# Opening of an attention-plus-MLP kernel: loads of two chunks at once, all scores of group 0 ahead of the MLP, and idle products between

## The chip, the cores and the metric

The kernel runs on one core of a Trainium2 chip. The metric is the device time of one execution in microseconds (us). Three executions of the kernel before gave a median of 213.64 us (213.39 to 215.62). The engines are named as the profile names them: PE is TensorE (its matrix products and transposes), PEld its weight loads, ACT is ScalarE, DVE is VectorE, POOL is GpSimd, SP is SyncE. POOL and SP issue the DMAs here: POOL every load, SP every store and every transposing DMA.

## The reference

Decaying linear attention over 4 batches, 8 heads, 768 positions and a head dimension of 64, followed by an MLP with an exact GELU over the 3072 tokens (512 to 2048 to 512). All inputs are float32.

```python
for b in range(nb):                       # blocks of 64 positions
    intra = einsum('bhic,bhjc->bhij', qb, kb) * Dmask
    intra = einsum('bhij,bhjd->bhid', intra, vb)
    inter = einsum('bhid,bhde->bhie', qb * lam_pow, kv_state)
    out[:, :, sl] = intra + inter
    kv_state = lam_block * kv_state + einsum('bhsd,bhse->bhde', kb * rev_pow, vb)
x = out.transpose(0, 2, 1, 3).reshape(B * S, H * D)
return gelu_exact(x @ w_in) @ w_out
```

## The kernel before

**Tiles.** The sequence is cut into 6 groups of 128 positions. A group has 4 chunks, one for each batch, so chunk n belongs to group n // 4. A chunk holds 128 positions of all 8 heads. The attention output of a group is a tile `x_t` of 128x4x512 (features by tokens), 128 columns for each chunk. The MLP of a group multiplies it with 16 slices of `w_in` (4 products of 128x512 each, one GELU on ACT behind them), and then with `w_out` (16 parts, "p0" to "p15", of 4 products each, for four chunks). All multiplications are in bf16; the loads turn float32 into bf16 on the way.

**Group 0 and the others.** Group 0 has no state before it. A chunk of it is made by `transposed` (k and q, each 16 small PE transposes into a PSUM bank and one copy out, by ACT or DVE, into `kqT`), `scores0` (8 products and two DVE multiplications with the mask), `outputs0` (8 products with v) and `empty` (one DVE multiplication into the chunk's columns of `x_t`). For the groups after it, `visit(f, d)` issues the scores and state products of chunk d, interleaved with the outputs of chunk f. Chunks 4 to 7 are transposed on PE (`both_transposed`), chunks from 8 on by transposing DMAs that SP issues (`dma_transposes`, L252 for k and L253 for q, called by `request`).

**The order is written out by hand.** `ask` (L126) issues loads on POOL's queue in the order of a string: "k0" is k of chunk 0, "v0" is v of chunks 0 and 1, "i0-3" slices 0 to 2 of `w_in` (two DMAs), "o0-4" a quarter of `w_out` (one DMA), "V1" v of all of group 1 (four DMAs). The loads of POOL count their landings on eight semaphores in turn, so that each load waits until the eighth load ahead of it has landed. The first string is at L143. `keep_warm(n)` issues n products of 128x512 on a tile of zeros, whose result nobody reads. `mlp(g, n2, n3)` returns the MLP of a group as named blocks: "a", "b" and "m" blocks compute slices of `w_in`, the slices below n3 without the columns of the group's last chunk, which "l" blocks add; `run_blocks` (L494) runs them in order and, ahead of a block, whatever the plan names for it.

**The opening of group 0** stands at L501 to L526: the first three chunks are transposed, chunks 0 and 1 are finished and the scores of chunk 2 made. The rest of group 0's attention hangs on MLP blocks (L565): `third` at b0 (outputs of chunk 2, transposes of chunk 3), scores of chunk 3 at m2, its outputs at m4. `ahead_of_group_1` at m5 issues POOL work: `decay_v(4)` (`vd`, the decayed values of chunk 4, which needs V1), loads k7 and q7, `decay_v(5)`, two copies, `decay_v(6)`, `decay_v(7)`, and then the loads V2, k8, q8, k9, q9. `visit(None, 4)` is at p6.

**Group 1** follows with the plan of `plan_of(1)` (L603 to L624; n is 8 there): `request(9)` at a0, stores of group 0's results and `request(10, 11)` at m5, `visit(None, 8)` at m7, `visit(8, 9)` at m12, `visit(9, 10)` at p2. `request(8)` stands at p14 of group 0. SP works its queue in order: the transposes of chunk 8, two stores, the transposes of chunk 9, two stores, those of chunks 10 and 11.

Of the kernel before, what the change touches and what calls it, by code (L numbers as in the profile page):

```python
# [9 lines left out]
BF16 = mybir.dt.bfloat16  # L10
ALU = mybir.AluOpType
ACT = mybir.ActivationFunctionType
# [3 lines left out]
def kernel(  # L16
# [28 lines left out]
    qkv_pool = ctx.enter_context(tc.tile_pool(name="qkv", bufs=10))  # L45
# [19 lines left out]
    raw = {}  # L65
    dram = dict(q=q, k=k, v=v)

    def load(n, name):
        g, b = n // B, n % B
        t = raw[n, name] = qkv_pool.tile([128, H, D], BF16, tag=name, name=f"{name}_t", bufs=10)  # L70
        nc.gpsimd.dma_start(t, dram[name][b, :, g * C:(g + 1) * C, :].rearrange("h si d -> si h d"))  # L71

    def load_pairs(n, name):
        g, b = n // B, n % B
        if n < B:
            t = raw[n, "kq"] if (n, "kq") in raw else qkv_pool.tile([128, H, 2, D], BF16, tag="kq", name="kq_t", bufs=B)
            raw[n, "kq"] = t
            t = t[half("kq".index(name))]  # L80
        else:
            t = raw[n, name] = qkv_pool.tile([64, H, 2, D], BF16, tag="q2", name="q2_t", bufs=B)
        src = dram[name][b, :, g * C:(g + 1) * C, :].rearrange("h (p j) d -> p h (j d)", j=2)
        nc.gpsimd.dma_start(t.rearrange("p h j d -> p h (j d)"), src)  # L84

    def load_parity(n):

        t = qkv_pool.tile([128, 2 * H, D], BF16, tag="v", name="v_t", bufs=2)
        src = v[n:n + 2, :, :C, :].rearrange("b h (p j) d -> j p (b h) d", j=2)
        for j in range(2):  # L90
            nc.gpsimd.dma_start(t[half(j)], src[j])  # L91
        for i in range(2):
            raw[n + i, "v"] = t[:, i * H:(i + 1) * H, :]

    def load_blocks(g):

        t = raw["group", g] = qkv_pool.tile([128, 2, B * HP, D], BF16, tag="vg", name="vg_t", bufs=3)
        src = v.rearrange("b (hp hi) s d -> hi s (b hp) d", hi=2)
        for u in range(2):
            for hi in range(2):  # L100
                s = g * C + u * L
                nc.gpsimd.dma_start(t[half(hi), u], src[hi, s:s + L])  # L102
# [4 lines left out]
    pos = consts.tile([128, 1], F32)  # L107
# [18 lines left out]
    def ask(items):  # L126

        for item in items.split():
            name, at = item[0], item[1:]
            if name in "kqv":  # L130
                n = int(at)
                if name == "v":
                    load_parity(n)
                elif n < B or n < 2 * B and name == "q":
                    load_pairs(n, name)
                else:
                    load(n, name)
            elif name == "V":
                load_blocks(int(at))
            else:  # L140
                (load_w_in if name == "i" else load_w_out)(*(int(x) for x in at.split("-")))

    ask("k0 q0 k1 q1 v0 k2 q2 i0-3 v2 k3 q3 i3-5 i5-8 i8-12 i12-16 o0-4 k4 q4 o4-8 V1 o8-12 k5 q5 o12-16 k6 q6")  # L143

    idle = consts.tile([128, 512], BF16)
    nc.vector.memset(idle, 0.0)
# [3 lines left out]
    warm = consts.tile([128, 1], F32)  # L150
# [28 lines left out]
    for hi in range(2):  # L179
        nc.vector.tensor_copy(ln_o[half(1 - hi), :, None], ln_r[half(1 - hi), :, hi:hi + 1])  # L180

    def make_lam_o(*hps):
        for hp in hps:
            nc.scalar.activation(lam_o[:, hp, :], row, ACT.Exp, scale=ln_o[:, hp:hp + 1])

    def make_dmask0():
# [3 lines left out]
    def make_lam():  # L190
        nc.scalar.activation(lam_k, ln[half(0)], ACT.Exp, scale=negp[half(0), 1:2])
        for hi in range(2):
            nc.scalar.copy(ln_h[half(hi), :, None], ln_r[half(hi), :, hi:hi + 1])
        for u in range(2):
            nc.scalar.activation(lam_v[:, u, :], ln_h, ACT.Exp, scale=negj[:, u:u + 1])
        nc.scalar.activation(lam_c, ln_h, ACT.Exp, scale=float(C))
# [12 lines left out]
    live = {}  # L209
    state = {}  # L210

    def begin(n):
        c = live[n] = Chunk()
        c.n, c.g, c.b = n, n // B, n % B
        if c.g:
            c.q, c.k = (raw.pop((n, name)) for name in "qk")
        else:
            c.kq = raw.pop((n, "kq"))
        c.v = of_group(n) if c.g else raw.pop((n, "v"))
        c.kqT = work_pool.tile([128, 2, HP, C], BF16, tag="kqT", name="kqT", bufs=6)  # L220
        c.kT, c.qT = c.kqT[:, 0], c.kqT[:, 1]
        return c

    def transposed(c, name, tag, eng):

        t_ps = bank([128, HP, C], BF16, tag, "t_ps")
        on = half("kq".index(name))
        for hp in range(HP):
            for j in range(2):
                for hi in range(2):  # L230
                    nc.tensor.transpose(t_ps[half(hi), hp, half(j)], c.kq[on, 2 * hp + hi, j, :], ident[on, on])  # L231
        if name == "k":
            dst, src = c.kT, t_ps
        else:
            dst, src = (t.rearrange(f"d hp ({o}) -> d hp p j", j=2) for t, o in ((c.qT, "p j"), (t_ps, "j p")))
        (nc.scalar.copy if eng is nc.scalar else eng.tensor_copy)(dst, src)  # L236
# [33 lines left out]
    def of_group(n):  # L270
        return raw["group", n // B][:, :, n % B * HP:(n % B + 1) * HP, :]
# [59 lines left out]
    def empty(c):  # L331
        nc.vector.tensor_mul(xT[c.g][:, :, c.b * C:(c.b + 1) * C], c.o, lam_o)  # L332
# [60 lines left out]
    def alloc_x(g):  # L393
        xT[g] = x_pool.tile([128, NK1, T], BF16, tag="x", name="x_t")
# [89 lines left out]

    idle_ps = {}

    def keep_warm(n, new=True):
        if new:
            idle_ps[0] = bank([128, 512], F32, "mo", "idle_ps")
        for _ in range(n):  # L490
            nc.tensor.matmul(idle_ps[0], idle[:, :128], idle, start=True, stop=True)


    def run_blocks(blocks, ahead):  # L494
        assert set(ahead) <= {name for name, _ in blocks}, set(ahead) - {name for name, _ in blocks}
        for name, run in blocks:
            for act in ahead.get(name, []):
                act()
            run()

    alloc_x(0)  # L501
    for n in range(3):
        begin(n)
    keep_warm(8)
    transposed(live[0], "k", "mh", nc.vector)
    make_dmask0()
    keep_warm(2, new=False)
    transposed(live[0], "q", "mo", nc.scalar)
    make_lam_o(0, 1)
    transposed(live[1], "k", "mh", nc.scalar)  # L510
    make_lam_o(2, 3)
    scores0(0)
    transposed(live[1], "q", "mo", nc.scalar)
    keep_warm(1)
    scores0(1)
    outputs0(0)
    empty(live[0])
    transposed(live[2], "k", "mh", nc.scalar)
    transposed(live[2], "q", "mo", nc.scalar)
    keep_warm(1)  # L520
    outputs0(1)
    empty(live[1])
    make_lam()
    scores0(2)
    nc.scalar.activation(warm, pos, ACT.Gelu)
    begin(3)  # L526


    alloc_x(1)

    def last_of_first():
        outputs0(3)
        empty(live[3])

    def third():
        outputs0(2)
        empty(live[2])
        transposed(live[3], "k", "mh", nc.scalar)
        transposed(live[3], "q", "mh", nc.scalar)

    def request(*ns):
        for n in ns:
# [2 lines left out]
    def same(n, eng):  # L545
        by_block(live[n], eng, None)
# [4 lines left out]
    def ahead_of_group_1():  # L551

        decay_v(4)
        ask("k7 q7")
        for n in range(B, 2 * B):
            begin(n)
        decay_v(5)
        same(5, nc.gpsimd)
        decay_v(6)
        decay_v(7)  # L560
        ask("V2 k8 q8 k9 q9")
        begin(8)
        begin(9)

    run_blocks(mlp(0, 2, 5), {  # L565
        "b0": [third],
        "m2": [lambda: scores0(3)],
        "m4": [last_of_first],
        "m5": [ahead_of_group_1],
        "m6": [make_dmask] + [lambda n=n: decay_k0(n, nc.vector) for n in range(B)],  # L570
        "p0": [first_states, lambda: by_block(live[4], nc.vector, nc.vector)],
        "p2": [lambda: both_transposed(live[4])],
# [104 lines left out]
```

## Time and profile before

| | us |
|---|---|
| median of three executions | 213.64 |
| the profiled execution, device time | 214.38 |
| its span, first to last instruction | 212.5 |
| PE busy in it | 203.6 |
| first PE product, on zeros | 1.19 |
| first product of the MLP (block a0) | 14.29 |
| first product of block m5 | 25.21 |
| last product with `w_in` of group 0 ends, state products of group 0 begin | 34.87 |
| `visit(None, 4)` begins on PE | 41.48 |
| `visit(9, 10)` begins on PE | 74.56 |

The profiled execution took 0.74 us longer than the median of the three. Its span leaves 1.88 us of the device time around the instructions. A line of the profile's timeline reads: start, duration, engine, line of the code, operation, tile written <- tiles read, form, count, and in brackets the idle time of the engine just before it and what ended it. The clock rows give the share of full speed that the TensorE clock was granted. Durations of products are modelled ends of pipelined work, so a row of products is best read by its start and the start of the next row.

### The profile page before, as it was taken

To read this page: it belongs to the slowest core of one execution; us is meant where nothing else is said; L and a number is where in the kernel's file an instruction comes from. 1 tells how busy PE (TensorE), PEld (TensorE's weight loads), DVE (VectorE), ACT (ScalarE), POOL (GpSimd) and SP (SyncE) were. 2 spreads that over 40 slices of the span, in tenths; PEclk is the share of its full clock that TensorE was granted. 3 is DMA by queue.
4 is the path that set the end of the run, shared out by engine and by line. 5 is a ranking of instruction groups with operands and counts; after the bars stand their busy time and mean duration, and the time that the engine had idled before them with its cause. 6 is when DMAs were issued, how large, how long until landed. Compare 5 with 4: busy or idle time off the path is not lost.

```text
span 212.5 us, 5560 instructions
## 1 busy us (share of the span) xinstructions
PE 203.6 (96%) x2408; PEld 102.7 (48%) x2408; DVE 84.7 (40%) x185; ACT 90.1 (42%) x166; POOL 103.9 (49%) x146
## 2 busy tenths in 40 slices
PE   7699999999999999999999999999999999999992
PEld 2456444555665454444444444444544444444462
DVE  3663663149736556627417525733330330000000
ACT  5563464247666411265412356321466211665121
POOL 8978464896999403999709994670000000000000
PEclk9855999999999999999999999999999999999999
DMA  6999999999999999999999999964100012100121
GB/s 60 141 175 201 204 186 177 188 98 144 95 195 211 116 150 110 71 141 203 178 100 105 132 255 114 148 94 157 51 3 0 3 74 77 49 0 0 49 81 70
DMA packets 94744, 24.48 MB, mean 115 GB/s; under 512 B 86912, under 2 KB 91776, under 8 KB 94720
## 3 DMA queue, kind: packets, MB, share of 16 engines
q0 software_dynamic: 73568, 13.64, 83.4%
q1 hardware_dynamic: 21152, 10.50, 28.1%
q8 instruction: 19, 0.31, 0.6%
q14 instruction: 5, 0.04, 0.1%
HBM read 27.27 MB, written 6.29 MB: 158 GB/s over the span
## 4 chain that ended last, share of the span: by engine, by line
PE 85%; DMA 8%; POOL 4%; ACT 1%; issue 1%; SPq 0%; POOLq 0%
PE o_ps L455 37%; PE h_ps L416 36%; DMA kqT<-q_t 4%; DMA v_t<-in_v_dram 3%; PE sc_ps L340 3%; PE o_ps L340 2%; POOL kq_t L84 2%; PE kv_ps L340 2%; PE o_ps L466 2%; POOL v_t L91 1%; PE h_ps L433 1%; PE t_ps L245 1%; POOL w_in_t L121 1%; ACT g_t L435 1%; PE t_ps L231 0%
## 5 line engine op out<-in xcount | busy, mean ns | idle before, releaser
L416 PE MATMUL h_ps<-x_t,w_in_t 128*128 128x512 bf16 (+3 forms) x400 | 86.6, 374 | 1.1 <-ACT g_t L435 0.7
L455 PE MATMUL o_ps<-w_out_t,g_t 128*128 128x512 bf16 x368 | 83.0, 380 | 0.0
L425 ACT ACTIVATE g_t<-h_ps 128x512 bf16<-128x512 f32 (+1 forms) x96 | 55.7, 585 | 33.4 <-PE h_ps L416 33.4
L416 PEld LDWEIGHTS <-w_in_t 128*128 128x128 bf16 x400 | 38.4, 100 | 42.8 <-issue 3.2
L455 PEld LDWEIGHTS <-g_t 128*128 128x128 bf16 x368 | 34.7, 98 | 40.3
L332 DVE TENSOR_TENSOR x_t<-o_ps,lam_o 128x512 bf16<-128x512 f32 x24 | 16.6, 691 | 71.2 <-PE o_ps L340 71.2
L444 ACT COPY o_sb<-o_ps 128x512 f32<-128x512 f32 (+1 forms) x25 | 14.2, 569 | 64.3 <-PE o_ps L455 61.8
L275 POOL TENSOR_TENSOR vd<-vg_t,lam_v 128x512 bf16<-128x512 bf16 x20 | 21.2, 1060 | 27.0 <-DVE t L301 11.8
L71 POOL DMA_DIRECT2D k_t<-in_k_dram x20 | 18.1, 903 | 0.3 <-issue 0.2
L102 POOL DMA_DIRECT2D vg_t<-in_v_dram x20 | 16.5, 842 | 3.1 <-DMA w_in_t<-in_moe_w_in_dram 2.3
L286 DVE TENSOR_TENSOR sm<-sc_ps,dmask 128x512 bf16<-128x512 f32 x20 | 13.7, 683 | 10.4 <-PE sc_ps L340 10.4
L262 POOL COPY k<-k_t 64x256 bf16<-64x256 bf16 x34 | 14.3, 421 | 1.0
L71 POOL DMA_DIRECT2D q_t<-in_q_dram x16 | 14.4, 900 | 0.0
L340 PEld LDWEIGHTS <-kqT 64*64 64x64 bf16 (+1 forms) x352 | 7.9, 109 | 10.0 <-issue 8.6
L340 PE MATMUL sc_ps<-kqT 64*64 64x64 bf16 (+1 forms) x352 | 11.0, 203 | 0.8 <-ACT kqT L236 0.6
L266 DVE COPY k<-k_t 64x256 bf16<-64x256 bf16 x34 | 10.8, 317 | 0.5
L311 DVE TENSOR_TENSOR state<-t,lam_c 128x256 bf16<-128x256 f32 x16 | 9.9, 618 | 0.6
L340 PE MATMUL o_ps<-sm,vg_t 64*64 64x64 bf16 x320 | 8.4, 193 | 0.0
L340 PE MATMUL kv_ps<-vd,k 64*64 64x64 bf16 x288 | 8.1, 193 | 0.0
L121 POOL DMA_DIRECT2D w_in_t<-in_moe_w_in_dram x10 | 6.4, 661 | 2.0 <-DMA w_in_t<-in_moe_w_in_dram 1.1
L340 PE MATMUL o_ps<-kqT,mid 64*64 64x64 bf16 x160 | 6.4, 194 | 0.5 <-issue 0.5
L340 PEld LDWEIGHTS <-vg_t 64*64 64x64 bf16 x320 | 6.8, 108 | 0.0
(73 smaller groups left out, 135.2 us busy)
## 6 DMA issues: line engine op xcount, KB each, us to landing
out_dram<-o_sb SPq DMA_DIRECT2D x23, 256.0 KB, 5.0
k_t<-in_k_dram POOLq DMA_DIRECT2D x20, 128.0 KB, 6.8
q_t<-in_q_dram POOLq DMA_DIRECT2D x20, 128.0 KB, 7.5
vg_t<-in_v_dram POOLq DMA_DIRECT2D x20, 128.0 KB, 10.4
w_out_t<-in_moe_w_out_dram POOLq DMA_DIRECT2D x4, 512.0 KB, 10.4
w_in_t<-in_moe_w_in_dram POOLq DMA_DIRECT2D x4, 256.0 KB, 8.2
w_in_t<-in_moe_w_in_dram POOLq DMA_DIRECT2D x4, 192.0 KB, 6.3
kq_t<-in_k_dram POOLq DMA_DIRECT2D x4, 128.0 KB, 4.7
```

What stands on the lines that cost most here:

```text
L71: nc.gpsimd.dma_start(t, dram[name][b, :, g * C:(g + 1) * C, :].rearrange("h si d -> si h d"))
L102: nc.gpsimd.dma_start(t[half(hi), u], src[hi, s:s + L])
L262: same.tensor_copy(c.k2[half(hi), hi], k_r[half(hi), :, hi, :])
L266: copy(c.k2[half(hi), 1 - hi], k_r[half(1 - hi), :, hi, :])
L275: nc.gpsimd.tensor_mul(vd[n], of_group(n), lam_vb)
L286: nc.vector.tensor_mul(c.sm, c.sc, dmask)
L332: nc.vector.tensor_mul(xT[c.g][:, :, c.b * C:(c.b + 1) * C], c.o, lam_o)
L340: nc.tensor.matmul(out_, lhsT, rhs, start=start, stop=True, skip_group_check=True)
L416: nc.tensor.matmul(hs[kf][:, lo:up], w_in_t[:, ki, kf * 128:(kf + 1) * 128], x_t[:, ki, lo:up], start=(ki == 0 and lo == 0), stop=(ki == N ...
L425: nc.scalar.activation(g_t[:, kf, :up], hs[kf][:, :up], ACT.Gelu)
L444: nc.scalar.copy(o_sb, ps_)
L455: nc.tensor.matmul(om[io], g_t[:, kf, io * C:(io + 1) * C], w_out_t[:, kf, :], start=(kf == 0), stop=(kf == NK2 - 1))
```

## The change

- `load_pairs` loads k (or q) of two chunks, n and n+1, with one DMA into a tile for both. In the string "k0" now stands for chunks 0 and 1, "q4" for chunks 4 and 5.
- The first string has all k, q and v of group 0 ahead of `w_in`, `w_in` in four pieces instead of five, and q5 and q7 are gone from the strings since q4 and q6 bring them.
- `transposed` puts k and q of a chunk into one PSUM bank of tag "mh"; before, q took one of "mo" (chunk 3 excepted).
- The opening goes by pairs of chunks. All scores and the outputs of chunks 0 to 2 stand ahead of the MLP, with 28 idle products between them in place of 12. The Gelu table is loaded ahead of the scores of chunk 2 rather than behind them.
- In the MLP of group 0, n3 is 3 in place of 5, the outputs of chunk 3 are at b0, and `ahead_of_group_1` is at m3.

```diff
-        src = dram[name][b, :, g * C:(g + 1) * C, :].rearrange("h (p j) d -> p h (j d)", j=2)
-        nc.gpsimd.dma_start(t.rearrange("p h j d -> p h (j d)"), src)
+        src = dram[name][b:b + 2, :, g * C:(g + 1) * C, :].rearrange("b h (p j) d -> p (b h) (j d)", j=2)
+        nc.gpsimd.dma_start(t.rearrange("p b h j d -> p (b h) (j d)"), src)
...
-    ask("k0 q0 k1 q1 v0 k2 q2 i0-3 v2 k3 q3 i3-5 i5-8 i8-12 i12-16 o0-4 k4 q4 o4-8 V1 o8-12 k5 q5 o12-16 k6 q6")
+    ask("k0 q0 v0 k2 q2 v2 i0-3 i3-6 i6-11 i11-16 o0-4 k4 q4 o4-8 V1 o8-12 k5 o12-16 k6 q6")
...
-        t_ps = bank([128, HP, C], BF16, tag, "t_ps")
+        if name == "k":
+            c.t_ps = bank([128, 2, HP, C], BF16, "mh", "t_ps")
+        t_ps = c.t_ps[:, "kq".index(name)]
...
     keep_warm(8)
-    transposed(live[0], "k", "mh", nc.vector)
+    transposed(live[0], "k", nc.vector)
     make_dmask0()
-    keep_warm(2, new=False)
-    transposed(live[0], "q", "mo", nc.scalar)
-    make_lam_o(0, 1)
-    transposed(live[1], "k", "mh", nc.scalar)
-    make_lam_o(2, 3)
+    transposed(live[1], "k", nc.scalar)
+    keep_warm(3)
+    transposed(live[0], "q", nc.scalar)
+    transposed(live[1], "q", nc.scalar)
+    make_lam_o()
+    keep_warm(1)
     scores0(0)
-    transposed(live[1], "q", "mo", nc.scalar)
     keep_warm(1)
     scores0(1)
+    keep_warm(3)
     outputs0(0)
     empty(live[0])
-    transposed(live[2], "k", "mh", nc.scalar)
-    transposed(live[2], "q", "mo", nc.scalar)
     keep_warm(1)
+    transposed(live[2], "k", nc.scalar)
+    transposed(live[3], "k", nc.scalar)
     outputs0(1)
     empty(live[1])
+    keep_warm(1)
+    transposed(live[2], "q", nc.scalar)
+    transposed(live[3], "q", nc.scalar)
     make_lam()
+    nc.scalar.activation(warm, pos, ACT.Gelu)
+    keep_warm(2)
     scores0(2)
-    nc.scalar.activation(warm, pos, ACT.Gelu)
-    begin(3)
+    keep_warm(2)
+    scores0(3)
+    keep_warm(3)
+    outputs0(2)
+    empty(live[2])
+    keep_warm(3)
...
-        ask("k7 q7")
+        ask("k7")
...
-    run_blocks(mlp(0, 2, 5), {
-        "b0": [third],
-        "m2": [lambda: scores0(3)],
-        "m4": [last_of_first],
-        "m5": [ahead_of_group_1],
+    run_blocks(mlp(0, 2, 3), {
+        "b0": [last_of_first],
+        "m3": [ahead_of_group_1],
```

More of the change, by code (lines that the diff above doesn't have):

```diff
@@ L77, in load_pairs @@
         if n < B:
-            t = raw[n, "kq"] if (n, "kq") in raw else qkv_pool.tile([128, H, 2, D], BF16, tag="kq", name="kq_t", bufs=B)
-            raw[n, "kq"] = t
+            t = raw[n, "kq"][0] if (n, "kq") in raw else qkv_pool.tile([128, 2, H, 2, D], BF16, tag="kq",
+                                                                        name="kq_t", bufs=2)
+            for i in range(2):
+                raw[n + i, "kq"] = (t, t[:, i])
             t = t[half("kq".index(name))]
         else:
-            t = raw[n, name] = qkv_pool.tile([64, H, 2, D], BF16, tag="q2", name="q2_t", bufs=B)
-        src = dram[name][b, :, g * C:(g + 1) * C, :].rearrange("h (p j) d -> p h (j d)", j=2)
-        nc.gpsimd.dma_start(t.rearrange("p h j d -> p h (j d)"), src)
+            t = qkv_pool.tile([64, 2, H, 2, D], BF16, tag="q2", name="q2_t", bufs=2)
+            for i in range(2):
+                raw[n + i, name] = t[:, i]
+        src = dram[name][b:b + 2, :, g * C:(g + 1) * C, :].rearrange("b h (p j) d -> p (b h) (j d)", j=2)
+        nc.gpsimd.dma_start(t.rearrange("p b h j d -> p (b h) (j d)"), src)
     def load_parity(n):
@@ L180, with make_lam_o @@
         nc.vector.tensor_copy(ln_o[half(1 - hi), :, None], ln_r[half(1 - hi), :, hi:hi + 1])
-    def make_lam_o(*hps):
-        for hp in hps:
+    def make_lam_o():
+        for hp in range(HP):
             nc.scalar.activation(lam_o[:, hp, :], row, ACT.Exp, scale=ln_o[:, hp:hp + 1])
@@ L217, in begin @@
         else:
-            c.kq = raw.pop((n, "kq"))
+            c.kq = raw.pop((n, "kq"))[1]
         c.v = of_group(n) if c.g else raw.pop((n, "v"))
@@ L222, in begin, with transposed @@
         return c
-    def transposed(c, name, tag, eng):
-        t_ps = bank([128, HP, C], BF16, tag, "t_ps")
+    def transposed(c, name, eng):
+        if name == "k":
+            c.t_ps = bank([128, 2, HP, C], BF16, "mh", "t_ps")
+        t_ps = c.t_ps[:, "kq".index(name)]
         on = half("kq".index(name))
@@ L485, with keep_warm @@
     idle_ps = {}
-    def keep_warm(n, new=True):
-        if new:
+    def keep_warm(n):
+        if not idle_ps:
             idle_ps[0] = bank([128, 512], F32, "mo", "idle_ps")
@@ L501 @@
     alloc_x(0)
-    for n in range(3):
+    for n in range(B):
         begin(n)
     keep_warm(8)
-    transposed(live[0], "k", "mh", nc.vector)
+    transposed(live[0], "k", nc.vector)
     make_dmask0()
-    keep_warm(2, new=False)
-    transposed(live[0], "q", "mo", nc.scalar)
-    make_lam_o(0, 1)
-    transposed(live[1], "k", "mh", nc.scalar)
-    make_lam_o(2, 3)
+    transposed(live[1], "k", nc.scalar)
[4 more added lines that the diff above has]
+    keep_warm(1)
     scores0(0)
-    transposed(live[1], "q", "mo", nc.scalar)
     keep_warm(1)
     scores0(1)
+    keep_warm(3)
     outputs0(0)
     empty(live[0])
-    transposed(live[2], "k", "mh", nc.scalar)
-    transposed(live[2], "q", "mo", nc.scalar)
     keep_warm(1)
+    transposed(live[2], "k", nc.scalar)
+    transposed(live[3], "k", nc.scalar)
     outputs0(1)
     empty(live[1])
+    keep_warm(1)
+    transposed(live[2], "q", nc.scalar)
+    transposed(live[3], "q", nc.scalar)
     make_lam()
+    nc.scalar.activation(warm, pos, ACT.Gelu)
+    keep_warm(2)
     scores0(2)
-    nc.scalar.activation(warm, pos, ACT.Gelu)
-    begin(3)
+    keep_warm(2)
[4 more added lines that the diff above has]
+    keep_warm(3)
     alloc_x(1)
@@ L533, in last_of_first @@
         empty(live[3])
[L535 to L539, printed above, removed]
     def request(*ns):
```

## The prediction

> **What bounds the kernel now.** I read the idle time of PE first, then the clock by stage, then backwards from the last place where PE waits for a DMA. PE is busy 203.6 of 212.5 us, and after 26 us its timeline has only three gaps: 0.48 us (51.9), 0.24 us (62.1) and this one, in group 1:
>
> ```profile
> 72.48 1.89 PE L455 MATMUL o_ps<-w_out_t,g_t 128*128 128x512 bf16 x8
> 74.56 0.22 PE L340 MATMUL sc_ps<-kqT 64*64 64x64 bf16 x2 [0.18 <-DMA kqT<-q_t]
> ```
>
> It is short, but its releaser is a DMA. `visit(9, 10)` waits for q of chunk 10, transposed by DMA, and gets it just as PE arrives. The chain of waits says the same; its pieces here read start, duration, what:
>
> ```profile
> 65.02 9.40 DMA kqT<-q_t
> 74.42 0.14 issue
> 74.56 0.22 PE sc_ps L340 x2
> ```
>
> So two chains meet at 74.4 us: PE's, and one of DMAs. What makes the DMA chain late? SP's own timeline (start, duration, issue) shows no pause from 54.00 on:
>
> ```profile
> 54.00 1.32 SPq L252 DMA_TRANSPOSE kqT<-k_t  x1
> 55.38 1.26 SPq L253 DMA_TRANSPOSE kqT<-q_t  x1
> 56.70 1.04 SPq L391 DMA_DIRECT2D out_dram<-o_sb  x2
> 57.84 2.21 SPq L252 DMA_TRANSPOSE kqT<-k_t  x1
> 60.10 1.50 SPq L253 DMA_TRANSPOSE kqT<-q_t  x1
> 61.64 1.20 SPq L391 DMA_DIRECT2D out_dram<-o_sb  x2
> 62.95 1.98 SPq L252 DMA_TRANSPOSE kqT<-k_t  x1
> 65.02 1.57 SPq L253 DMA_TRANSPOSE kqT<-q_t  x1
> ```
>
> Its first entry waited for k of chunk 8 (landed 53.91 by the trace's landing records). POOL issued that load (47.58) behind this work:
>
> ```profile
> 37.80 1.04 POOL L275 TENSOR_TENSOR vd<-vg_t,lam_v 128x512 bf16<-128x512 bf16 x1 [0.94 <-DMA vg_t<-in_v_dram]
> 38.79 0.92 POOL L71 DMA_DIRECT2D k_t<-in_k_dram  x1
> 39.71 0.70 POOL L84 DMA_DIRECT2D q_t<-in_q_dram  x1
> ...
> 44.33 3.28 POOL L102 DMA_DIRECT2D vg_t<-in_v_dram  x4
> 47.58 0.92 POOL L71 DMA_DIRECT2D k_t<-in_k_dram  x1
> ```
>
> POOL stood still until V1 had landed (37.63) and then worked without a pause to 51.1. V1 stood in a DMA queue that is never empty from 3 to 44 us. Nothing in this chain (loads, V1, POOL, V2 and k8, SP, q10) waits for PE: the PE results that SP's entries need, such as the outputs of chunk 4 (47.8) for 62.95, are long there. The profile puts a few of SP's durations down to PE; by the program's own waits they are SP's.
>
> The opening itself, where the change works, runs half the time at half clock (columns: stretch, its length, busy time and count of PE, then of four other engines, granted clock, DMA share, GB/s):
>
> ```profile
> 5.22:8.64 3.42, 2.39 (x65) 1.42 (x59) 2.11 (x3) 2.05 (x6) 3.42 (x6) 1.00 1.71 133
> 8.64:12.05 3.41, 2.50 (x49) 1.79 (x48) 2.62 (x5) 1.29 (x4) 3.41 (x6) 0.50 1.51 166
> 18.88:22.29 3.41, 3.41 (x21) 1.43 (x20) 1.29 (x2) 1.25 (x3) 2.71 (x4) 0.50 1.25 205
> 22.29:25.70 3.41, 2.91 (x36) 1.94 (x36) 2.84 (x6) 1.75 (x4) 1.63 (x2) 1.00 1.23 205
> ```
>
> The clock changes at 8.64 and 22.29, four steps of 3.41 us apart. A step in which PE was 70% busy was followed by half clock; after three steps of 73 to 91% it stayed there; a step that was busy throughout brought it back; steps of 85% kept it.
>
> **The loads.** Bytes and row lengths are the same; four loads take the place of eight. In the queue's busy time, k or q of one chunk lands about 0.74 us after the load ahead. Two halves of `w_in` of 192 KB land 0.97 us apart (11.29, 12.26), two of 128 KB 0.65 us (16.24, 16.89): 5.05 and 5.08 ns a KB, so no fixed part a load, and merging saves 0. The Trainium skill, "DMA: Bandwidth & Descriptors", section "Anatomy of one DMA — SWDGE (gpsimd) path", gives each DMA a fixed cost of about 2.0 us; by that, four loads fewer would be worth up to 8 us one after the other. The row shows it hidden by the loads in flight, and the row decides. The first load, of 1024 rows, is issued in about 1.05 us in place of 0.86 (the 1024-row v loads take 0.82 to 0.88, the 512-row ones 0.70): +0.2 for all behind it. All loads of group 0 and i0-3 together land when q3 did, 17.46, so 17.7; before, i0-3 alone was there at 14.15. i6-11 ends between the old 20.75 (i5-8) and 24.61 (i8-12), by bytes 23.6.
>
> **The opening on PE.** 28 idle products in place of 12. At half clock eight took 3.60 us, so 16 more cost 7.2 us at half and 3.5 at full clock (their gap at 25 to 35 us, 0.22). They lie where PE waits for loads and copies anyway: PE now has nothing but attention until 17.7. From the first transposes at about 5.8 (k0 and k1 in one load) at half clock throughout, with transposes at 0.55 us for sixteen, scores 0.5, outputs 0.5 and idle 0.43, the chain of these and the copies ends near 20.8; at full clock the loads end last. So a0 starts between 17.7 and 20.8. I take 17.7: at half clock PE would be busy without a gap from 5.8 on, and the 18.88 row says that one such step brings the clock back. Copies (0.58 on ACT), masks (1.29 a chunk on DVE), `make_lam_o` in one piece (1.4) and the Gelu table (1.28) end by about 17, under the loads. One bank for k and q of a chunk waits for copies two chunks back, done by then.
>
> From a0 on everything is at full clock: 44 products took 9.66 us (25.21 to 34.87), so 64 take 14.05; the outputs of chunk 3 add 0.3 (0.64 at half clock); fewer split slices about nothing. m6 comes at 17.7 + 0.3 + 6 x 0.88 = 23.3, so the wait for i6-11 is 0.3, up to 1. The state products begin at 32.35 to 33.0 in place of 34.87: PE is 1.9 to 2.5 us ahead. If a0 starts at 20.8, it is at 35.15, 0.3 behind.
>
> **From there to 74.4.** q5 now comes with q4 ahead of V1: V1 lands 0.2 + 0.74 later, 38.6. POOL's q7 issue (0.70) between `vd` and V2 falls away; the pair q6, q7 is issued ahead of `vd` while POOL waits for V1 anyway, at no cost (0.85 if V1 were there already). So V2 and k8 shift by 0.2 + 0.74 - 0.70 = +0.24. `vd` of chunk 4 is ready at 39.7; `visit(None, 4)` needs it 0.37 us after its start, at 41.85 before, so PE's lead is cut to at most 2.1 us there. SP's chain follows k8: q10 at 74.66, by +0.24. PE arrives at 72.3 to 72.5 and waits about 2.2 us. After 75.4 PE has no gap to the end, so the end moves with `visit(9, 10)`: 212.5 + 0.24 = 212.7 of span, 214.6 of device time against 214.38; put on the median, 213.64 + 0.24 = 213.9.
>
> How firm is +0.24? A landing is that of the slowest of 16 DMA engines: V1 landed at 37.63 where the fifteenth stood at 36.7, k8 at 53.91 where it stood at 52.3, each behind instruction fetches of 16 KB that held one engine for some 1.0 us (14.2, 22.5, 49.5). Where these fall in the new kernel I can't tell: -2.6 if neither lags, +1.3 for one more. I take none.
>
> **The rivals.** (1) The wait costs the clock. A wait of 2.2 us leaves a step of 3.41 us at 36 to 68% busy; 70% lost the clock at 8.64. The step after it then runs at half rate: 3.41 / 2 = 1.7 us, so 213.9 + 1.7 = 215.6, slower than before. It decides once the wait exceeds about 1 us (30% of a step); against it, the 70% were mostly small products, and 86% (49.6 to 53.0) kept it. The Trainium skill, "TensorE: Matmul & The Clock Gate", section "Why this matters for your kernels", only asks for no idle gaps over about 3 us; by that this wait costs nothing and the time is 213.9. The trace lost the clock with no gap longer than 1.03 us.
>
> (2) The DMA chain moves ahead with PE (no laggard at V1 or k8, at most 2.6): PE's lead is kept, 213.64 - 2.1 = 211.5. For it: the lag is chance. Against it: same bytes, same queue, and 20 us of SP issues behind it.
>
> (3) The opening doesn't do what it says: clock lost between idle products, a0 near 20.8, and the first step of the MLP at half rate: 35.15 + 1.7 against 34.87, PE 2.0 behind, no wait at 74.4, 215.6. For it: 70 to 91% busy was not enough before.
>
> **How the numbers follow.** Forecast (chain fixed, +0.24, clock kept) 0.48, its own range 212.6 to 215.2 (the +1.3 above, and its like below); rival 1 0.18; rival 2 0.20; rival 3 0.14. The range reaches to rival 2's 211.5 and a little over the 215.6 of rivals 1 and 3: 211.4 to 216.2. One per cent, which is about what a measurement of this kernel tells from no change, is 2.1 us: under 211.5 lies about half of rival 2 and of the forecast's lower tail, 0.20; over 215.8 half of rivals 1 and 3 and a tail, 0.24; the rest 0.56.
>
> **What would show it.** Right: a0 at 17 to 18.5 at full clock, m5 earlier than 25.2 by its own slices, PE 1.5 to 2.5 us ahead at the state products, V1 at 38 to 39, k8 at 53.5 to 55, and a PE gap of 1 us or more, released by a transposing DMA, around 72 to 75. Rival 1 shows 0.5 in the clock row behind that gap; rival 3 shows 0.5 after a0. Wrong: PE ahead at 75 by more than k8 is, or a landing of V1 that follows from the merged loads.

## The result and the profile after

| | before | changed |
|---|---|---|
| device time, median (lowest to highest) | 214.38 us (213.12 to 216.31), 20 runs | 213.09 us (212.25 to 216.71), 20 runs |
| ratio to before, 95% interval | | 0.9941 (0.9916 to 0.9965) |
| the profiled execution | 214.38 us, span 212.5 | 213.61 us, span 211.7 |

The changed kernel is 0.6% faster, 1.3 us at the median. It was run twice more, each time beside the kernel before in the same job: 0.9920 (0.9889 to 0.9951) and 0.9957 (0.9920 to 0.9994). The forecast was 0.1% slower; the time lies in its range, on the other side of no change. Now the views that the forecast was built on, after the change.

The opening by clock steps, changed kernel (columns as before: stretch, its length, busy time and count of PE, of PE's weight loads, of DVE, ACT and POOL, granted clock, DMA share, GB/s):

```profile
5.03:8.44 3.41, 1.91 (x64) 1.26 (x66) 1.56 (x2) 0.69 (x2) 3.41 (x5) 1.00 2.02 160
8.44:11.86 3.42, 2.94 (x35) 1.34 (x29) 2.01 (x4) 2.24 (x6) 2.08 (x4) 0.50 1.92 176
11.86:15.27 3.41, 3.16 (x87) 2.06 (x88) 1.86 (x3) 1.84 (x4) 1.83 (x3) 1.00 1.76 183
```

A step in which PE was busy 1.91 of 3.41 us (56%) was followed by half clock, as before; and here the clock came back after one step at half, 86% busy, where before it took four. The MLP's first product starts at 18.20 at full clock (forecast 17.7 to 20.8, taken 17.7) and the state products at 32.68 (forecast 32.35 to 33.0; the first of them before at 34.80, 34.87 being the end of the product ahead of it). PE is 2.1 us ahead there.

GpSimd, from the landing of V of group 1 on (start, duration, engine, line, operation; in brackets the idle time ahead of it and what ended it):

```profile
36.66 1.04 POOL L282 TENSOR_TENSOR vd<-vg_t,lam_v 128x512 bf16<-128x512 bf16 x1 [2.11 <-DMA vg_t<-in_v_dram]
37.65 0.92 POOL L71 DMA_DIRECT2D k_t<-in_k_dram  x1
38.58 1.05 POOL L282 TENSOR_TENSOR vd<-vg_t,lam_v 128x512 bf16<-128x512 bf16 x1
...
42.67 3.30 POOL L107 DMA_DIRECT2D vg_t<-in_v_dram  x4
45.93 0.93 POOL L71 DMA_DIRECT2D k_t<-in_k_dram  x1
```

V1 landed at 36.5, 1.1 us earlier than before; the forecast had it 0.94 later. q7 is gone from this stretch, and V2 is issued at 42.67 in place of 44.33: 1.7 us earlier, where the sum said 0.24 later. SyncE follows:

```profile
52.59 1.29 SPq L259 DMA_TRANSPOSE kqT<-k_t  x1
53.93 1.25 SPq L260 DMA_TRANSPOSE kqT<-q_t  x1
...
61.38 2.04 SPq L259 DMA_TRANSPOSE kqT<-k_t  x1
63.51 1.44 SPq L260 DMA_TRANSPOSE kqT<-q_t  x1
```

It starts 1.4 us earlier (54.00 before). q of chunk 10, issued at 63.51 (65.02 before), landed at 70.6 in place of 74.42, by the trace's landing records. At `visit(9, 10)` PE comes 2.3 us after it, at 72.93, and no longer waits. The chain of waits there and at the place of the lead's first loss (start, duration, what):

```profile
49.71 1.19 issue
...
71.20 1.73 PE o_ps L462 x8
72.93 0.15 PE sc_ps L347 x2
...
73.45 0.34 issue
73.79 0.19 PE kv_ps L347
```

So of the 2.1 us that PE is ahead, waits called "issue" take some: 1.19 us at 49.71 (0.48 at the same place before), 0.34 at 73.45 and 0.70 at 132.84. PE is 0.5 us ahead at the end. The section on the hardware says what these waits are.

### The profile page after: what moved, and what is told of

Its sections match the earlier page's. It is cut to its first block, busy times and chain, and to the rows that moved or that the text cites. A ratio compares the mean times of both kernels' runs of the same rounds, so it can differ in the third digit from the quotient of the medians.

```text
span 211.7 us, 5538 instructions
## 1 busy us (share of the span) xinstructions
PE 199.5 (94%) x2387; PEld 101.2 (48%) x2416; DVE 86.5 (41%) x185; ACT 90.1 (43%) x165; POOL 99.4 (47%) x138
## 4 chain that ended last, share of the span: by engine, by line
PE 91%; issue 3%; DMA 3%; ACT 1%; POOL 1%; POOLq 0%
PE h_ps L423 39%; PE o_ps L462 37%; PE sc_ps L347 4%; DMA kq_t<-in_q_dram 3%; PE o_ps L347 3%; PE idle_ps L498 2%; PE kv_ps L347 2%; PE o_ps L473 2%; PE h_ps L440 1%; PE t_ps L238 1%; PE t_ps L252 1%; ACT kqT L243 1%; PE t_ps L248 0%; POOL kq_t L89 0%; ACT g_t L442 0%
## 5 line engine op out<-in xcount | busy, mean ns | idle before, releaser
L423 PE MATMUL h_ps<-x_t,w_in_t 128*128 128x512 bf16 (+3 forms) x388 | 83.4, 366 | 0.8 <-ACT g_t L442 0.2
L462 PE MATMUL o_ps<-w_out_t,g_t 128*128 128x512 bf16 x354 | 80.5, 379 | 1.8 <-issue 1.6
L423 PEld LDWEIGHTS <-w_in_t 128*128 128x128 bf16 x400 | 37.6, 98 | 41.0 <-issue 0.4
L498 PE MATMUL idle_ps<-idle 128*128 128x512 bf16 x25 | 9.3, 494 | 1.3 <-DVE idle L151 1.2
L318 DVE TENSOR_TENSOR state<-t,lam_c 128x256 bf16<-128x256 f32 x16 | 9.4, 585 | 0.5
L312 DVE CAST mid<-t 128x256 bf16<-128x256 f32 x12 | 7.3, 608 | 0.4
```

The source lines that it names most:

```text
L423: nc.tensor.matmul(hs[kf][:, lo:up], w_in_t[:, ki, kf * 128:(kf + 1) * 128], x_t[:, ki, lo:up], start=(ki == 0 and lo == 0), stop=(ki == N ...
L462: nc.tensor.matmul(om[io], g_t[:, kf, io * C:(io + 1) * C], w_out_t[:, kf, :], start=(kf == 0), stop=(kf == NK2 - 1))
```

## The experiments

All ratios are to the kernel before, run on the same chip in the same job, with 95% intervals. Two readings stood against each other. LOADS, the forecast's: the end follows the chain of loads (V1, GpSimd, V2, SyncE's transposes). TENSOR, called CODE in the first four expectations: PE's own work sets the end, less what it waits for its own instructions.

**The changed kernel again** (no edit).

> The changed kernel once more, with a second trace. Theory CODE (PE is 2.1 us ahead after the opening and loses part of it where its next 256 instructions are not there yet): PE ahead by 1.9 to 2.3 us at the state products again; waits of PE without a data releaser at the same instructions as in the first trace (end of visit(5, 6), visit(9, 10), a visit of group 4), of another size, 0.2 to 1.5 us each; time 212.3 to 213.6. Theory LOADS (the end follows the transposed q of chunk 10): that q lands just as PE reaches visit(9, 10) again, and the end moves with it.

0.9920 (0.9889 to 0.9951). Its profiled execution took 216.78 us and is worth reading: the clock row stayed at 0.50 from 8.15 to 21.81, the MLP began at 22.31 and the state products at 36.78, 2.0 us later than before. PE was busy throughout in four steps at half clock, as the profile counts it, and only the fourth was followed by full clock (columns as above):

```profile
8.15:11.57 3.42, 3.42 (x50) 1.76 (x45) 1.59 (x3) 2.25 (x6) 2.40 (x5) 0.50 1.92 174
14.98:18.40 3.42, 3.42 (x47) 1.64 (x45) 0.93 (x2) 2.35 (x9) 3.00 (x4) 0.50 1.27 204
18.40:21.81 3.41, 3.41 (x22) 1.15 (x21) 2.51 (x5) 1.50 (x3) 1.87 (x4) 0.50 1.19 207
21.81:25.20 3.39, 3.39 (x40) 2.46 (x39) 1.89 (x4) 1.15 (x3) 1.43 (x2) 1.00 1.21 207
```

The opening that the forecast's third rival describes is thus real in single executions; it is not the median. Of the 42 executions of the changed kernel five have a mean granted clock of 0.965 or 0.968, as this one, and took 215.6 to 216.8 us; the others have 0.98 or more.

**80 more PE instructions.** The lead stays, the place of every later instruction in the program moves.

```
     keep_warm(8)
+    fill(40)          # 40 products, 64 columns wide, on the idle tile
     transposed(live[0], "k", nc.vector)
```

> 40 tiny products in the first wait of PE move every later instruction 80 places on in the stream. CODE: the places 256 apart fall on large products in place of visits, the three waits (1.2, 0.3, 0.7 us in the first trace) shrink to under 0.3 in all, and the time falls by 0.8 to 1.8 us against the changed kernel. LOADS: no change (within 0.3 us), since the load chain is not touched.

0.9932 (0.9898 to 0.9965): no gain. In its profile the clock was full from 4.96 on and PE 2.4 to 3.0 us ahead until 53, the best opening with nothing left out. It was lost to two kinds of wait: instructions (0.73 us at 53.03, 0.81 at 80.51) and the load chain, as here at chunk 9:

```profile
67.97 0.22 PE L347 MATMUL sc_ps<-kqT 64*64 64x64 bf16 x2 [0.89 <-DMA kqT<-q_t]
```

At the end PE was 0.2 us behind the kernel before.

**The twenty idle products of the gaps narrowed.**

```
-    def keep_warm(n):
+    def keep_warm(n, cols=32):
...
-            nc.tensor.matmul(idle_ps[0], idle[:, :128], idle, start=True, stop=True)
+            nc.tensor.matmul(idle_ps[0][:, :cols], idle[:, :128], idle[:, :cols], start=True, stop=True)
...
-    keep_warm(8)
+    keep_warm(8, 512)
```

> The 20 idle products behind the first eight are 32 columns wide in place of 512, so PE is no longer kept busy in the gaps; the count of instructions is the same. If the clock is what the opening gains: half clock from about 8.5 us until one to three steps of 3.41 us after the MLP's start, PE 1.7 to 4 us later at the state products, time up by 1 to 3 us. LOADS: time up by less than 0.5 us, as PE's lead is worth nothing. If the order alone gains: within 0.3 us.

0.9905 (0.9870 to 0.9940), no slower than with the wide ones. Its groups of 32 transposes took 1.06 us at 6 to 14 us, where the changed kernel's took 0.69 at full clock, and the trace's first record of the clock, at full, is at 20.64; but the opening was shorter by the idle work itself, so the MLP began at 17.09 and the state products at 33.17. In this trace, what the wide products win in clock they cost in time.

**The same order, k and q one chunk a load.**

```
-        src = dram[name][b:b + 2, :, g * C:(g + 1) * C, :].rearrange("b h (p j) d -> p (b h) (j d)", j=2)
-        nc.gpsimd.dma_start(t.rearrange("p b h j d -> p (b h) (j d)"), src)
+        for i in range(2):
+            src = dram[name][b + i, :, g * C:(g + 1) * C, :].rearrange("h (p j) d -> p h (j d)", j=2)
+            nc.gpsimd.dma_start(t[:, i].rearrange("p h j d -> p h (j d)"), src)
```

> The changed kernel with one load for each chunk's k and q, in the same order of bytes. The forecast's step (no fixed part to a load): every landing within 0.3 us, time within 0.4 us. If merging is what brought V1 from 37.6 to 36.5: V1 0.7 us or more later, and the time up by 0.3 to 1 us where something waits for it.

0.9962 (0.9928 to 0.9996). About half of the gain is gone, though the interval overlaps that of the changed kernel. Not all of it lies in the kernel's own work: between first and last instruction the median of `single_loads` is 211.0 us and that of `again` 210.45, and the rest of the 1.0 us between their device times is outside. The trace is clearer than the time. V1 landed at 37.4 and V2 was issued at 43.61, and the wait that the forecast was about is back:

```profile
73.73 0.22 PE L348 MATMUL sc_ps<-kqT 64*64 64x64 bf16 x2 [0.85 <-DMA kqT<-q_t]
```

Why do the same bytes in the same order come later? The rates, three stretches of 3 us each (the last column is GB/s). Before:

```profile
6.00:9.00 3.00, 1.82 (x57) 1.22 (x52) 1.86 (x3) 2.41 (x7) 3.00 (x5) 0.94 1.86 139
9.00:12.00 3.00, 2.25 (x46) 1.64 (x47) 2.26 (x4) 0.88 (x2) 3.00 (x6) 0.50 1.46 167
12.00:15.00 3.00, 2.63 (x33) 1.54 (x28) 1.58 (x3) 2.74 (x9) 1.89 (x4) 0.50 2.01 170
```

The changed order with single loads:

```profile
6.00:9.00 3.00, 2.11 (x36) 1.20 (x34) 0.82 (x1) 1.26 (x3) 3.00 (x5) 0.73 1.88 140
9.00:12.00 3.00, 3.00 (x21) 1.07 (x20) 2.02 (x4) 1.67 (x5) 3.00 (x6) 0.50 1.73 162
12.00:15.00 3.00, 3.00 (x51) 1.71 (x50) 1.34 (x3) 0.86 (x2) 1.95 (x4) 0.64 1.88 166
```

The changed kernel:

```profile
6.00:9.00 3.00, 2.21 (x67) 1.53 (x68) 1.56 (x2) 1.13 (x3) 3.00 (x5) 0.91 2.14 164
9.00:12.00 3.00, 2.79 (x20) 1.07 (x20) 2.15 (x4) 1.69 (x6) 1.62 (x4) 0.52 1.93 176
12.00:15.00 3.00, 2.75 (x84) 2.03 (x84) 1.72 (x3) 1.57 (x4) 1.73 (x3) 1.00 1.78 184
```

With pairs the DMA engines move 164, 176 and 184 GB/s, with single loads 140, 162 and 166. Pairs against single loads in the same order, over 9 us, that is 3 us x (24 + 14 + 18) = 0.17 MB, or 0.8 us at the 205 GB/s of the stretch behind. The bytes landed by 16 us say the same over all 17 traces: 1.94 to 1.98 MB in the four with single loads, 2.10 to 2.15 MB in the thirteen with pairs. Merging pays some 0.8 us at the transfers, in the first 15 us alone.

**Each half of the change alone.** First the opening with the old loads and their old places:

```
-    ask("k0 q0 v0 k2 q2 v2 i0-3 i3-6 i6-11 i11-16 o0-4 k4 q4 o4-8 V1 o8-12 k5 o12-16 k6 q6")
+    ask("k0 q0 k1 q1 v0 k2 q2 i0-3 v2 k3 q3 i3-5 i5-8 i8-12 i12-16 o0-4 k4 q4 o4-8 V1 o8-12 k5 q5 o12-16 k6 q6")
...
-        ask("k7")
+        ask("k7 q7")
```

(`load_pairs` as before too.)

> The opening of the changed kernel with every load as in the kernel before: one chunk each, the same places in the queue. ORDER says that the gain is the opening on the tensor engine alone, and that merging the loads is worth nothing: the ratio to the kernel before is that of the changed kernel, 0.992 (0.989 to 0.995), and in the trace the state products start 1.5 to 2.2 us ahead of the kernel before (34.87). BOTH says that each half brings a part, the merged loads because the load chain runs earlier: the ratio lies half-way, 0.996, and transposed q of chunk 10 lands at 73 to 75 us and is waited for. LOADS ALONE says 1.000. With the loads late the opening could also wait for k and q of chunk 3, which lie behind w_in's first blocks here: then the lead is under 1 us at the state products.

1.0178 (1.0131 to 1.0226), 4.4 us slower at the median; all three theories missed by far, and what the expectation named last is the reason:

```profile
17.40 0.44 PE L234 MATMUL t_ps<-ident,kq_t 64*64 64x64 bf16 x16 [2.41 <-DMA kq_t<-in_k_dram]
```

The opening wants k of chunk 3, which lies behind `w_in`'s first blocks there. PE stood 2.41 us, the clock fell to half until 24.8, and the MLP began at 25.39. Now the new loads with the old opening: `load_pairs` and both strings of the changed kernel, nothing else.

> The kernel before with the loads of the changed kernel (pairs, all of group 0 ahead of w_in), the opening as before. ORDER says 1.000 within 0.3%: the tensor engine goes its old way and the loads it waits for come no earlier than it needs them. LOADS says 0.994: the load chain (V of group 1 landed at 37.63 before) lands about 1 us earlier, at 36.2 to 36.7, transposed q of chunk 10 before 73 us, and the wait for it at 74.4 goes. What the trace shows of V's landing decides whether the pairs make the chain earlier at all: 36.2 to 36.7 says yes, 37.1 to 37.6 no.

1.0045 (1.0012 to 1.0078), 1.0 us slower by the ratio and 1.5 at the median. The chain did come earlier (V1 36.2, V2 issued 42.34, q of chunk 10 at 70.6), but the old opening wants `w_in` at 15 us, and that now lies behind all of group 0:

```profile
17.58 1.65 PE L420 MATMUL h_ps<-x_t,w_in_t 128*128 128x256 bf16 x7 [2.62 <-DMA w_in_t<-in_moe_w_in_dram]
```

PE is 1.4 us late from there. The halves need each other: one takes the loads that the other asks for.

**PE made shorter in the kernel before.** A part of the MLP's first product in group 0 is left out: ten products are 32 columns wide in place of 512. Counted beforehand as 2.1 us of PE's time, they are worth less: in the changed kernel PE goes from the MLP's first product to the state products in 13.30 us in all three traces with this edit, and in 14.47 or 14.48 in the nine with the changed opening, without this edit, whose MLP ran at full clock. That is 1.2 us, and every expectation below that counts 2.1 counts too much.

```
             for ki in range(NK1):
+                if g == 0 and kf > 10 and ki in (1, 2):
+                    nc.tensor.matmul(hs[kf][:, :32], w_in_t[:, ki, kf * 128:(kf + 1) * 128], x_t[:, ki, :32],
+                                     start=False, stop=False, skip_group_check=True)
+                    continue
```

> The kernel before with the tensor engine about 2.1 us shorter in group 0's MLP and nothing else changed: in group 0 ten of w_in's products (slices 11 to 15, row blocks 1 and 2) are 32 columns wide in place of 512, so part of the first matrix product of the MLP is left out; the number of instructions stays. LOADS, the forecast's reading, says that the wait for transposed q of chunk 10 grows by what the tensor engine is early, up to 2 us, and the end moves by at most 0.3 us (ratio 0.999 to 1.000). TENSOR says that the kernel is bound by the tensor engine's own work and that the end comes 1.2 to 2.1 us earlier (ratio 0.990 to 0.994).

1.0000 (0.9968 to 1.0032). The interval reaches 0.7 us down, where 1.2 us less would be 0.994: PE's work brought nothing that can be measured, as LOADS said. PE was 1.1 us ahead at the state products and lost it all by 81 us, 0.4 to its own instructions at 50.80 and most of the rest here:

```profile
74.86 0.22 PE L340 MATMUL sc_ps<-kqT 64*64 64x64 bf16 x2 [1.15 <-DMA kqT<-q_t]
```

**The load chain made later in the changed kernel.** The four multiplications stand behind the decay for chunk 7, do it over, and hold back the loads of V2.

```
         decay_v(7)
+        for _ in range(4):
+            nc.gpsimd.tensor_mul(vd[7], of_group(7), lam_vb)
         ask("V2 k8 q8 k9 q9")
```

> The changed kernel with four more multiplications on GpSimd ahead of its decay of v for chunk 7, which are done over afterwards: the last loads of group 1 and all transposing transfers behind them start about 4 us later, the tensor engine's work is untouched. Were the load chain what sets the end, it would be 4 us later than the changed kernel (ratio to the kernel before 1.011). TENSOR with slack says that the chain has about 2.3 us to spare at transposed q of chunk 10 (landed 70.6, wanted at 72.9) and less for those behind it, so 1 to 2.5 us come through (ratio 0.997 to 1.004), as waits for kqT and q at 72 to 76 us. NO CHAIN says none comes through (0.992).

1.0139 (1.0085 to 1.0193), median 216.62. Against the changed kernel's 0.992 to 0.996 that is 1.8 to 2.2%, or 3.9 to 4.7 us (2.7 to 5.8 with the interval): by the ratio all of the added 4.4 comes through. The profiled execution shows where, and that it need not be all:

```profile
42.88 4.46 POOL L573 TENSOR_TENSOR vd<-vg_t,lam_v 128x512 bf16<-128x512 bf16 x4
47.28 3.30 POOL L107 DMA_DIRECT2D vg_t<-in_v_dram  x4
```

```profile
76.22 0.22 PE L347 MATMUL sc_ps<-kqT 64*64 64x64 bf16 x2 [1.73 <-DMA kqT<-q_t]
```

PE waits 0.56, 1.05 and 1.73 us for q of chunks 8, 9 and 10. This execution took 215.80, the fastest of six, and its span is 2.0 us over that of the changed kernel: there the slack of 2.3 us was real. In the others it must have been smaller or none, if the chain is what made them longer; none of them was traced.

**PE made shorter in the changed kernel** (the edit of before_short).

> The changed kernel with the tensor engine about 2.1 us shorter in group 0's MLP, by the same edit as in before_short: ten of w_in's products 32 columns wide in place of 512, so a part of the MLP's first product is left out. LOADS says that in most executions the load chain (V of group 1, GpSimd's decay, V of group 2, SyncE's transposing transfers) sets the end of the changed kernel too: the ratio stays at 0.990 to 0.993, and the wait for transposed q of chunk 10 or 9 shows in the trace. TENSOR says 2.1 us less: 0.982 to 0.984. BOTH, the two within a microsecond of each other, says 0.985 to 0.990.

0.9899 (0.9861 to 0.9937): 0.2 to 0.6% below the three runs of the changed kernel, 0.5 to 1.2 us, where the edit takes 1.2 from PE. Here PE's work is worth something, where in the kernel before nothing could be measured; the intervals overlap. LOADS wanted a wait for a transposed q in the trace, and there is none: PE is 1.9 us ahead of the kernel before at the state products and 2.2 us at the end, so in this execution PE's own work set the end.

**V of group 1 asked for earlier**, to move the chain the other way:

```
-    ask("... o0-4 k4 q4 o4-8 V1 o8-12 k5 o12-16 k6 q6")
+    ask("... o0-4 k4 q4 V1 o4-8 o8-12 k5 o12-16 k6 q6")
```

> The changed kernel with V of group 1 asked for ahead of w_out's blocks 4 to 8 (0.5 MB, 2.2 us at the rate of the trace) in place of behind them; nothing else. LOADS says that the chain comes 1.5 to 2.2 us earlier (V of group 1 landed at 34.3 to 35.5, V of group 2 issued at 40.5 to 41.5) and that the end follows as far as the tensor engine lets it: 0.5 to 1.5 us below the changed kernel, ratio 0.985 to 0.990, with no wait for kqT of over 0.3 us in the trace. TENSOR says no gain: 0.991 to 0.994. If w_out's blocks 4 to 8 come too late (wanted at 37.6), the tensor engine waits there and it is slower than the changed kernel.

0.9954 (0.9919 to 0.9990): no gain. V1 landed at 35.1, but the chain was not earlier:

```profile
40.41 0.85 POOL L269 COPY k<-k_t 64x256 bf16<-64x256 bf16 x2 [2.09 <-DMA k_t<-in_k_dram]
41.34 2.22 POOL L282 TENSOR_TENSOR vd<-vg_t,lam_v 128x512 bf16<-128x512 bf16 x2
43.51 3.31 POOL L107 DMA_DIRECT2D vg_t<-in_v_dram  x4
```

GpSimd went on to wait for k of chunk 5, which lies behind two blocks of `w_out`, and V2 was issued at 43.51, 0.8 us later than in the changed kernel, and PE waited for q of chunk 10 again, 1.40 us until 74.72. The step meant to test LOADS did not happen. Two runs were made on top of it, one with PE shorter (the ten narrow products again, part left out), one with the narrow idle products.

> Both edits, V of group 1 ahead and the ten narrow products (part of the MLP's first product is left out). LOADS WITH TENSOR CLOSE BEHIND says that now both limits move and the end with them: 1.5 to 2.1 us below the changed kernel, ratio 0.982 to 0.985, while each edit alone gives less than half of that. TENSOR says the same as for the narrow products alone. LOADS ALONE says the same as for V ahead alone.

0.9941 (0.9910 to 0.9971).

> V of group 1 ahead of w_out's blocks 4 to 8, and the twenty idle products in the gaps 32 columns wide in place of 512. If the idle products hold the clock to some use, this is slower than V ahead alone; if they are worth nothing, the same within 0.3%, and with a narrower spread (none of the executions 2 us above the median that the changed kernel had).

0.9975 (0.9944 to 1.0006); the highest of its twelve runs was 215.04. Neither is apart from V ahead alone.

**V1 and k of chunk 5 ahead**, beside the changed kernel once more on the same chip:

```
-    ask("... k4 q4 o4-8 V1 o8-12 k5 o12-16 k6 q6")
+    ask("... k4 q4 V1 o4-8 k5 o8-12 o12-16 k6 q6")
```

> The changed kernel once more, on the chip of the two below, as their measure. Both theories: ratio 0.991 to 0.995, V of group 1 landed at 36.2 to 37.1 and V of group 2 issued at 42.3 to 43.3 in its trace.

0.9957 (0.9920 to 0.9994).

> The changed kernel with V of group 1 ahead of w_out's blocks 4 to 8 and k of chunk 5 ahead of blocks 8 to 12. With V ahead alone GpSimd went on to wait for k of chunk 5 (2.09 us, until 40.41), so V of group 2 was issued no earlier. LOADS says that without that wait V of group 2 is issued at 41.0 to 41.7, transposed q of chunk 10 lands 1 to 1.5 us earlier than in the changed kernel, and the end follows by 0.4 to 1.2 us, as far as the tensor engine lets it: 0.4 to 0.6% below the changed kernel on the same chip. TENSOR says no gain (within 0.2%).

0.9922 (0.9895 to 0.9949). V2 was issued at 41.07, as expected, and no wait for a transposed chunk is left; the time is 0.35% lower than beside it, less than the intervals can tell.

> The same with ten of w_in's products of group 0 32 columns wide in place of 512 (a part of the MLP's first product is left out; 2.1 us of the tensor engine). TWO LIMITS CLOSE TOGETHER says that with both earlier the end comes 1.2 to 2 us below the changed kernel (0.6 to 1.0%), and at least 0.5 us below V ahead without the narrow products. LOADS ALONE says as V ahead without them (within 0.2%).

0.9914 (0.9883 to 0.9946), 0.4% below again2, where 0.6 to 1.0% was expected. PE was 4.05 us ahead of the kernel before at the state products and V2 was issued at 39.95, so both limits had moved. At 48 us the lead met the third:

```profile
48.02 0.20 PE L347 MATMUL kv_ps<-vd,k 64*64 64x64 bf16 x2
50.01 0.22 PE L347 MATMUL o_ps<-kqT,mid 64*64 64x64 bf16 x2 [1.80 <-issue]
```

No version of these is apart from the changed kernel by more than the intervals.

## Why the prediction was off

*Two chains meet at 74.4 us and the loads bind.* Right for the kernel before: 1.2 us taken from PE there left the time at 1.0000, with most of the lead lost to this wait.

*The opening on PE.* Right in its numbers (18.20, 32.68, lead 2.1), but partly by luck. The forecast had the loads end last, at 17.7; the first slices of `w_in` were there at 16.82, and PE came to them at 18.20 without waiting for a load. Its rule for the clock, that one step busy throughout brings it back, fails both ways: 86% was enough here, and in `again` three steps busy throughout were not. So PE's busy share alone doesn't tell when the clock returns. The profile is also one of the better ones: over the ten traces with the changed opening and nothing left out of the MLP (`order_only` aside) the state products start at 32.4 to 36.8, with 33.4 to 33.6 in the middle, a lead of 1.3.

*The load chain, +0.24.* This is the step that failed, in its first term, +0.94 for V1. With pairs V1 landed at 36.0 to 37.5 in eight traces (mean 36.6), with single loads at 37.1 to 37.6 in four (mean 37.4): 0.8 us earlier where the sum had 0.94 later. About half of this miss of 1.7 is "merging saves 0", as the run with single loads shows: 37.42 there, 36.6 with pairs. That reading compared halves of 192 KB that landed at 13.16 and 14.15 with halves of 128 KB that landed at 18.20 and 18.77, by the landing records 5.2 and 4.5 ns a KB. The DMA engines moved 170 GB/s in the one stretch and 202 in the other, so the two say nothing of a part that each load costs, and the first of the merged loads run earlier still, at 139 GB/s. The other half is not merging. In `single_loads` q5 lies ahead of V1, and its price is there (from the landing of `w_out`'s first quarter to that of V1 9.1 us, in the kernel before 8.2), but that first quarter landed 1.1 us earlier than before, 28.30 against 29.44. The forecast had nothing for this, and no run separates the new order of the loads from `w_in` in fewer pieces. The second term, q7's issue for -0.70, held: from V1's landing to V2's issue it is 0.6 us less. V2 was issued at 42.7 (mean of seven) in place of 44.0 (mean of four): -1.3 in place of +0.24.

*The end moves with the chain.* With -1.3 in place of +0.24 the forecast's own sum would give 1.3 us less; measured were 1.3, 1.6 and 0.65. The agreement is no proof. In the changed kernel the wait of 2.2 us that the forecast had at 74.4 is gone, and in none of its three traces does PE wait for a transposed chunk; there the end is that of PE's lead less what its other waits take. The mechanism held when the chain was made later (GpSimd's 4.4 us came through by the ratio). For this change it ended where the chain came ahead of PE.

*The bound on luck.* The forecast allowed -2.6 to +1.3 for where a lagging engine falls, and took none. q of chunk 10 took 9.40 us to land before and 7.1 after; over thirteen other traces it took 7.1 to 9.2. Part of the 3.8 us by which it came earlier in the profiled pair is such luck, and the median shows 1.3.

*The rivals.* (2) named what happened, the loads moving ahead with PE, with too high a price: 2.1 us against 1.3. Its reason, no laggard, holds for V1 in the profiled pair, where the last of the 16 DMA engines came 0.93 us after the fifteenth before (36.70, 37.63) and 0.09 after (36.40, 36.49). It isn't the whole: over the traces the fifteenth itself came at 36.3 with pairs (mean of eight) and at 36.9 with single loads (mean of four). (1) fell with pool_late, where a wait of 1.73 us left the step from 74.33 on 45% busy, and the next one still ran at full clock (columns as in the opening):

```profile
74.33:77.74 3.41, 1.52 (x69) 1.04 (x70) 0.59 (x1) 0.00 (x0) 0.00 (x0) 1.00 1.59 127
77.74:81.20 3.46, 3.46 (x18) 1.57 (x17) 2.52 (x8) 0.58 (x1) 0.00 (x0) 1.00 1.75 155
```

The 70% and 56% that were followed by half clock at 8.6 and 8.4 us were no rule for later. The Trainium skill, "TensorE: Matmul & The Clock Gate", section "Why this matters for your kernels", asks for no gaps over about 3 us; here it agrees with the row, as it did not in the opening. (3) is what the long execution of `again` shows. The Trainium skill, "DMA: Bandwidth & Descriptors", section "Anatomy of one DMA — SWDGE (gpsimd) path", which the forecast set aside, gives each load a fixed cost of about 2.0 us. The runs agree with its direction, in the first 15 us alone, at 0.8 us for four loads fewer, or 0.2 a load. The forecast's row of `w_in` had been taken too far.

*What stays open.* Whether PE or the loads end last in the median execution of the changed kernel: lengthening the chain costs all of it by the ratio, though 2.0 us of 4.4 in the one trace, and shortening PE, the chain or both brings at most 0.2 to 0.6%, within the intervals. And why pairs move faster early: fewer issues in the way, more packets under way, or both. The profile shows 1.8 packets a DMA engine under way at 5 to 7 us with pairs and 1.3 with single loads, which fits either. With pairs `w_in`'s first load is issued at 7.98, with single loads in the same order at 10.14.

## What to carry to other kernels

A rate read where a queue is full says nothing of the time when it is filling: price merged loads from the rows of the stretch in which they run. When two chains meet within a microsecond, shorten each one alone before you believe either, and when a change has two halves, try each alone: here both lost, because each needs what the other moves. An edit that brings one transfer forward moves the wait to the next one that the same engine needs, as k of chunk 5 took the place of V1. And measure what an edit takes away before you weigh its result: ten narrow products were counted as 2.1 us and took 1.2.

## What the runs showed of the hardware

PE waits for its own instructions. The page's queue of instruction fetches reads, for the changed kernel:

```profile
q8 instruction: 19, 0.31, 0.6%
```

That is 16 KB a fetch, and for PE's some 4,800 instructions about 253 a fetch. PE's longer waits called "issue" stand at instructions 1217, 1985 and about 3521, in the kernel before at 1218, and with 80 instructions more at 1474 and 2241: all but the third, whose place is known to a few, 193 or 194 past a multiple of 256. A fetch held one DMA engine for 0.9 to 2.0 us, and in the changed kernel PE went on 1.5 to 2.2 us after it ended. The first of these waits, near 50 us, was 0.5 to 0.9 us in ten of the 17 traces, 1.19 in the changed kernel's, and 1.80 where PE came earliest; in the other five there is none over 0.3. That these are fetches is read from places and times; no run took one away. The Trainium skill, "Runtime: NRT & Kernel Launch", section "Instruction fetch mechanics", has the 256 instructions and 16 KB, which the places here agree with, and calls the cost of crossing such a boundary mostly hidden. In twelve of the 17 traces 0.5 to 1.8 us of it was not.

The clock's record needs a second look at the durations. The page of the narrowed idle products shows full clock from the start, but its 32 transposes took 1.06 us at 6, 11.5 and 13.2 us, and those of the changed kernel 0.69 to 0.76 at full clock. The trace's own records of the clock begin at 20.64 there, so the page's 1.00 ahead of that is no measurement.
